# Places of results named by the planner, eight score products on eight parts of the array, and a new written order

## The chip, the core and the metric

The kernel runs on one core of a Trainium2 chip. Its engines are TensorE (PE, products; PEld is its weight load), VectorE (DVE), ScalarE (ACT), GpSimd (POOL) and SyncE (SP, which issues all the transfers here). The metric is the time of one execution in microseconds; the kernel before takes 1485.46 us (median of 3 runs, 1484.67 to 1485.84).

## The reference, cut to what matters

An attention with packed keys feeds two feed-forward layers. With 8 batches, 8 heads, 576 tokens, head size 64 and 32 packed rows:

```
def sm_attn(qq, kk, vv):
    s = scale * qq @ kk^T;  a = softmax(s);  return a @ vv
p_packed = sm_attn(p, k, v)              # 32 rows per batch and head
x = sm_attn(q, p_packed, p_packed)       # 4608 tokens x 512
h = x @ w_in;  g = (a0 + a1 h + a2 h^2 + a3 h^3) / (1 + |b0||h| + |b1|h^2 + 1e-6)
x2 = g @ w_out                           # 512 -> 2048 -> 512
h = x2 @ w_in2;  out = (h - tanh(h)) @ w_out2
```

All weights arrive as 64-bit words and are brought to two 32-bit parts (high and low) on the chip; products of the layers are three passes (high by low, low by high, high by high).

## The kernel before, in words

The first attention is done in 16 units `u` (a batch and four of its heads). A unit is a chain over engines: `sc` (scores, PE), `mx` (row maximum, DVE), `ex` (exp, ACT), `et` (transposes, PE), `ta` (ACT), `av` (times v, PE), `y` (ACT), `bt` (transposes, PE), `bd` (ACT), and `z` (the sums' reciprocals, DVE). In `sc` the keys lie with two heads in the two halves of the partitions, and 288 tokens of the 576 make one result bank: eight products of 64 rows by 32 columns of weights, four for the first half of the tokens and then four for the second, on the same four parts of the array.

The second attention is folded into the first layer: `g` multiplies the packed rows of a batch with a 256-wide piece of `w_in` (`gH`, `gL` split its result), `sm` makes the scores of a block of tokens, `si sx ss se sz sn so sh sl` their softmax and split. The tokens stand in 10 blocks of 384 or 512, each with 8 steps; step `g` (0 to 79) is `l1` (PE, hidden values), `ft fu fw` (ACT), `f2 f3` (DVE), `fq` (POOL or DVE), `r` (ACT), `b0 b1 b2` (DVE), `b3` (POOL or DVE), and the second product in two parts: `l2h` needs `b0`, `l2l` needs `b3`. The weights come as `raw` (two buffers), are turned by `d1` (ACT or DVE), `dA` (ACT) and `d` (DVE), and are split by `wh` (ACT) and `w2`, `w3`, `w4` (POOL or DVE). After the 80 steps come the last layer's products `l3`, `l4`, `m3`, `m4`.

The results of `sc et av g sm l1` take turns in a ring "h" of two places in the result memory, each two banks. `l3` opens other banks in the same memory, behind the last `f3`.

Every engine works through its own queue in order. The order of all 3965 pieces of work is written out in a table, `ORDER`, of such names (a `+` sets the second of two possible engines); a class `Plan` walks through it and issues each piece, and where the table has nothing ready it would choose by costs and due times. An entry of the table thus fixes what stands in front of it on its engine, and nothing more.

Of the kernel before, what the change touches and what calls it, by code (L numbers as in the profile page):

```python
# [26 lines left out]
v.0 v.1 k.0 k.1 p.0 raw.0.0 raw.0.1 raw.1.0 id raw.1.1 dA.0 d1.0+ q.0 d.0 raw.2.0 dA.1 sc.0 sc.1 mx.0 d1.1+ ex.0  # L27
raw.2.1 mx.1 et.0 ex.1 et.1 d.1 raw.3.0 ta.0 z.0 av.0 ta.1 y.0 av.1 dA.2 z.1 bt.0 y.1 bd.0 d1.2+ bt.1 bd.1 sm.0 c
raw.3.1 d1.3 g.0.1 d.2 si.0 sx.0 ss.0+ p.1 open_t dA.3 d.3 se.0 sz.0 gH.0.1 k.2 sn.0+ raw.4.0 raw.4.1 gL.0.1 d1.4 sc.2
g.0.0 mx.2 dA.4 ex.2 so.0 d.4 w1d.0 sh.0 gH.0.0 wh.4.0 raw.5.0 raw.5.1 sl.0+ g.0.2 gL.0.0 w2.0+ wh.4.1 dA.5 l1.0 cabs  # L30
w1d.1 w2.1+ d1.5+ gH.0.2 raw.6.0 d.5 fu.0 gL.0.2 et.2 ft.0 fw.0 z.2 f2.0 raw.6.1 f3.0 g.0.3 ta.2 raw.7.0 fq.0 l1.1 r.0
d1.6+ dA.6 ft.1 b0.0 d.6 v.2 gH.0.3 gL.0.3 wh.6.1 l2h.0 av.2 w2.3+ fu.1 f2.1 wh.6.0 raw.7.1 w2.2 fw.1 f3.1 y.2 dA.7
b1.0 fq.1+ k.3 p.2 g.0.4 gH.0.4 b2.0 b3.0 bt.2 bd.2 w1d.2 w1d.3 raw.8.0 gL.0.4 sc.3 l1.2 d1.7 mx.3 r.1 ex.3 raw.8.1
d.7 ft.2 b0.1 fu.2 w1.1.0 b1.1 d1.8+ dA.8 d.8 fw.2 f2.2 et.3 l2l.0 fq.2 raw.9.0 ta.3 f3.2 wh.8.0 l2h.1 w2.4+ raw.9.1
wh.8.1 w2.5+ l1.3 z.3 q.1 g.0.5 r.2 d1.9 b2.1 b0.2 ft.3 fu.3 dA.9 b3.1+ fw.3 raw.10.0 b1.2 f2.3 gH.0.5 d.9 f3.3
raw.10.1 fq.3 l2l.1 gL.0.5 d1.10 b2.2 l1.4 b3.2+ v.3 av.3 dA.10 k.4 d.10 raw.11.0 fu.4 ft.4 f2.4 y.3 wh.10.1 wh.10.0
l2h.2 fw.4 bt.3 bd.3 f3.4 w2.7+ r.3 w2.6+ sc.4 raw.11.1 sm.1 dA.11 mx.4 p.3 w1d.5 si.1 l2l.2 fq.4 ex.4 b0.3 raw.12.0
d1.11 b1.3 r.4 d.11 b2.3 et.4 l1.5 ta.4 fu.5 raw.12.1 k.5 ft.5 dA.12 b3.3 z.4 sx.1 f2.5 g.0.6 v.4 f3.5 gH.0.6 d1.12
ss.1 l2h.3 raw.13.0 gL.0.6 b0.4 fw.5 raw.13.1 d.12 sc.5 se.1 av.4 y.4 bt.4 w1d.7 wh.12.0 bd.4 mx.5 ex.5 l2l.3 wh.12.1
w2.8+ et.5 w1d.6 v.5 b1.4 fq.5+ l1.6 dA.13 w2.9+ sz.1 d1.13 ta.5 fu.6 b2.4 g.1.0 ft.6 gH.1.0 d.13 f2.6 gH.1.1 wh.13.0  # L40
wh.13.1 raw.14.0 gL.1.0 r.5 f3.6 z.5 b3.4 l2h.4 fw.6 g.0.7 gL.1.1 gH.0.7 av.5 w2.11 raw.14.1 w2.10+ sn.1+ fq.6 gL.0.7
so.1 y.5 dA.14 d1.14 bt.5 b0.5 d.14 k.6 l2l.4 w1d.4 v.6 bd.5 sh.1 b1.5 r.6 b2.5 sl.1 sc.6 l1.7 fu.7 ft.7 l2h.5 mx.6
wh.14.0 f2.7 f3.7 raw.15.0 raw.15.1 ex.6 b3.5+ w2.12+ et.6 d1.15 wh.14.1 l1.8 b0.6 dA.15 d.15 w1.1.2 w2.13+ fw.7 ta.6
ft.8 z.6 l2l.5 av.6 wh.15.0 wh.15.1 p.4 l2h.6 f2.8 fq.7 fu.8 y.6 w2.15+ w2.14 r.7 rx f3.8 b1.6 bt.6 fw.8 b0.7 b2.6
b1.7 fq.8+ bd.6 b3.6 l1.9 g.1.2 ft.9 f2.9 gH.1.2 fu.9 gL.1.2 gH.1.3 l2h.7 f3.9 b2.7 l2l.6 b3.7+ fw.9 fq.9+ k.7 l1.10
r.8 ft.10 l2l.7 sp.0.0 fu.10 gL.1.3 b0.8 b1.8 sp.0.1 b2.8 f2.10 fw.10 w1.1.4 l1.11 l2h.8 fq.10+ ft.11 f3.10 g.1.4
fu.11 f2.11 r.9 gH.1.4 st.0.1 f3.11 b3.8 st.0.0 b0.9 b1.9 l2l.8 q.2 w1.1.6 v.7 sc.7 gH.1.5 b2.9 r.10 l2h.9 gL.1.4
gL.1.5 fw.11 sm.2 mx.7 b3.9 fq.11 ex.7 si.2 r.11 l2l.9 et.7 sx.2 l1.12 ta.7 ft.12 fu.12 b0.10 av.7 l2h.10 b1.10 ss.2+
b2.10 fw.12 z.7 y.7 se.2 f2.12 bt.7 f3.12 b3.10 bd.7 fq.12+ r.12 sz.2 l1.13 g.1.6 b0.11 l2l.10 gH.1.6 k.8 b0.12 ft.13
fu.13 b1.11 gL.1.6 gH.1.7 fw.13 f2.13 l2h.11 sn.2 fq.13 f3.13 gL.1.7 l1.14 b2.11 r.13 b3.11+ so.2 b1.12 fu.14 l1.15  # L50
# [233 lines left out]
class Plan:  # L284

    SIGNAL = {"PE": 200, "ACT": 150, "DVE": 130, "POOL": 135}

    IDLE, WARM = 1200, 3400
    PORT = ("DVE", "POOL")

    ALT = 600
    alts = {}
# [29 lines left out]
    def run(self):  # L328
# [131 lines left out]
def packed_attention_moe_kernel(  # L460
# [622 lines left out]
    EARLY = 4  # L1083
# [938 lines left out]
```

## Time and profile before

| | |
|---|---|
| three runs, median | 1485.46 us |
| the profiled execution | 1483.95 us, span 1482.2 us, mean granted clock 0.988 |
| PE | 1436.9 us busy, 97% of the span |
| DVE | 1237.0 us, 83% |
| ACT | 897.5 us, 61% |
| POOL | 280.5 us, 19% |
| DMA | 257.87 MB, mean 174 GB/s |

The times of the working below are those of the profiled execution; 1.75 us of it lie outside the span. An average over the span hides that its stretches have different limits: the table of 40 slices on the page shows DVE at nine tenths and over from about 75 us to about 700 us, PE below that only in the first slices and once in the middle, and DMA above eight tenths in the first two slices. A time in a timeline row is that of the first instruction of the row, and the number after it how long the row's instructions took together.

### The profile page before, as it was taken

To read this page: it belongs to the slowest core of one execution; us is meant where nothing else is said; L and a number is where in the kernel's file an instruction comes from. 1 tells how busy PE (TensorE), PEld (TensorE's weight loads), DVE (VectorE), ACT (ScalarE), POOL (GpSimd) and SP (SyncE) were. 2 spreads that over 40 slices of the span, in tenths; PEclk is the share of its full clock that TensorE was granted. 3 is DMA by queue.
4 is the path that set the end of the run, shared out by engine and by line. 5 is a ranking of instruction groups with operands and counts; after the bars stand their busy time and mean duration, and the time that the engine had idled before them with its cause. 6 is when DMAs were issued, how large, how long until landed. Compare 5 with 4: busy or idle time off the path is not lost.

```text
span 1482.2 us, 21855 instructions
## 1 busy us (share of the span) xinstructions
PE 1436.9 (97%) x8448; PEld 1191.6 (80%) x8448; DVE 1237.0 (83%) x1588; ACT 897.5 (61%) x1235; POOL 280.5 (19%) x168
## 2 busy tenths in 40 slices
PE   4789999999999999999989999999999999999998
PEld 1668888877899888888978888888888888888887
DVE  4899999999999999999978876797588657977785
ACT  4898777767776777677976543454355324543353
POOL 0232322113112322333210223201220112020000
PEclk8899999999999999999999999999999999999999
DMA  8873322232331313131236889587566566575563
GB/s 299 296 255 129 131 76 98 77 144 98 131 128 58 107 57 114 58 136 43 72 122 215 238 260 335 190 296 260 199 237 229 196 221 244 197 260 199 213 210 131
DMA packets 75000, 257.87 MB, mean 174 GB/s; under 512 B 7184, under 2 KB 25744, under 8 KB 60048
## 3 DMA queue, kind: packets, MB, share of 16 engines
q1 hardware_dynamic: 74896, 256.47, 49.9%
q8 instruction: 67, 1.10, 0.3%
q14 instruction: 37, 0.30, 0.1%
HBM read 204.02 MB, written 52.43 MB: 173 GB/s over the span
## 4 chain that ended last, share of the span: by engine, by line
PE 90%; DVE 4%; ACT 3%; issue 1%; DMA 1%; SPq 0%; DVEq 0%; ACTq 0%
PE acc L961 24%; PE acc L1296 19%; PE b L1296 17%; PE h L948 13%; PE b L1081 9%; PE h L801 3%; PE acc L1121 1%; PE acc L1122 1%; PE acc L1123 1%; PE h L724 1%; PE h L769 1%; DMA raw<-in_w_dram 1%; DVE t L986 1%; PE h L754 1%; DVE m L1009 0%
## 5 line engine op out<-in xcount | busy, mean ns | idle before, releaser
L948 PE MATMUL h<-ah,slot 128*128 128x320 f32 (+3 forms) x1024 | 214.8, 304 | 0.0
L961 PE MATMUL acc<-gh,slot 128*128 128x512 f32 (+1 forms) x800 | 172.7, 367 | 0.6 <-DVE gh L1003 0.6
L948 PEld LDWEIGHTS h<-ah,slot 128*128 128x128 f32 x1024 | 170.7, 193 | 1.1
L961 PEld LDWEIGHTS acc<-gh,slot 128*128 128x128 f32 x800 | 143.5, 188 | 30.7 <-issue 10.7
L961 PE MATMUL acc<-raw,slot 128*128 128x512 f32 (+1 forms) x720 | 165.4, 379 | 0.0
L961 PEld LDWEIGHTS acc<-raw,slot 128*128 128x128 f32 x720 | 130.2, 188 | 29.9 <-issue 9.2
L948 PE MATMUL h<-al,slot 128*128 128x192 f32 (+3 forms) x512 | 150.7, 308 | 2.7 <-DVE slot L813 1.5
L1335 ACT ACTIVATE yh<-slot 128x512 fp32r<-128x512 f32 x140 | 88.2, 631 | 79.7 <-PE b L1296 25.4
L1339 DVE TENSOR_TENSOR yl<-slot,yh 128x512 fp32r<-128x512 f32 x140 | 97.9, 714 | 19.6 <-ACT yh L1335 19.0
L971 ACT ACTIVATE t<-h,coa 128x1024 f32<-128x1024 f32 (+1 forms) x80 | 89.2, 1118 | 37.9 <-PE h L948 31.8
L975 ACT ACTIVATE u<-h 128x1024 f32<-128x1024 f32 (+1 forms) x80 | 74.9, 936 | 51.8 <-PE h L948 37.9
L948 PEld LDWEIGHTS h<-al,slot 128*128 128x128 f32 x512 | 98.3, 192 | 9.5 <-issue 4.8
L986 DVE TENSOR_TENSOR t<-t,h 128x1024 f32<-128x1024 f32 (+1 forms) x80 | 88.5, 1108 | 15.2 <-ACT t L971 10.2
L990 DVE SCALAR_TENSOR_TENSOR t<-t,coa,h 128x1024 f32<-128x1024 f32 (+1 forms) x80 | 93.7, 1171 | 2.9 <-ACT u L975 1.0
L961 PE MATMUL acc<-gl,slot 128*128 128x384 f32 (+1 forms) x400 | 91.9, 372 | 2.5 <-DVE gl L1012 2.5
L983 POOL TENSOR_TENSOR m<-u,r 128x1024 f32<-128x1024 f32 (+1 forms) x27 | 58.4, 2162 | 166.3 <-DVE t L986 46.6
L1081 PE MATMUL b<-xh,slot 128*128 128x512 f32 x256 | 83.3, 399 | 6.4 <-DVE t L990 6.4
L1335 ACT ACTIVATE yh<-ex 128x512 fp32r<-128x512 f32 x84 | 53.0, 632 | 52.0 <-PE acc L1296 18.7
L961 PEld LDWEIGHTS acc<-gl,slot 128*128 128x128 f32 x400 | 72.0, 190 | 14.5 <-issue 3.6
L1296 PE MATMUL acc<-yh,rg 128*128 128x512 f32 x256 | 78.8, 389 | 0.0
L1296 PE MATMUL acc<-yh,raw 128*128 128x512 f32 x256 | 78.8, 389 | 0.0
L1296 PE MATMUL b<-slot,rg 128*128 128x512 f32 x336 | 77.5, 389 | 0.0
(218 smaller groups left out, 3259.0 us busy)
## 6 DMA issues: line engine op xcount, KB each, us to landing
raw<-in_w_dram SPq DMA_DIRECT2D x64, 512.0 KB, 4.5
w<-w1d SPq DMA_DIRECT2D x28, 1024.0 KB, 4.8
raw<-w4d SPq DMA_DIRECT2D x28, 1024.0 KB, 5.1
rg<-w4d SPq DMA_DIRECT2D x28, 1024.0 KB, 5.2
rg<-w3d SPq DMA_DIRECT2D x12, 1024.0 KB, 5.1
raw<-w3d SPq DMA_DIRECT2D x12, 1024.0 KB, 5.0
k<-in_kT_dram SPq DMA_DIRECT2D x16, 576.0 KB, 5.4
out_dram<-o SPq DMA_DIRECT2D x36, 256.0 KB, 5.6
```

The costliest lines, as they stand in the source:

```text
L801: pe.matmul(out=ps[32 * hp:32 * hp + 32, i, :], lhsT=pp[b][r, hp, :], rhs=x[r, hp, :])
L948: pe.matmul(out=ps[:, f, t], lhsT=x, rhs=y, start=(i == 0), stop=(i == len(seq) - 1))
L961: pe.matmul(out=acc_t[n][m][:, 0:XW[n]], lhsT=w2_slot[2 * p + f][:, o:o + 128], rhs=x[:, f, :], start=(p == 0 and part == 512 and f == 0), ...
L971: act.activation(out=t_t[g], in_=hv(g), func=AF.Identity, scale=a3, bias=a2)
L975: act.activation(out=u_t[g], in_=hv(g), func=AF.Abs)
L983: by.tensor_tensor(out=q_m[g], in0=u_t.pop(g), in1=r_t[g], op=ALU.mult)
L986: dve.tensor_tensor(out=t_t[g], in0=t_t[g], in1=hv(g), op=ALU.mult)
L990: dve.scalar_tensor_tensor(out=t, in0=t, scalar=a1, in1=hv(g), op0=ALU.add, op1=ALU.mult)
L1081: pe.matmul(out=hy(b, f), lhsT=a, rhs=w, start=(j == 0), stop=(j == len(seq) - 1))
L1296: pe.matmul(out=to, lhsT=a, rhs=b, start=(first and n == 0 and i in (1, 6, 7, 5)), stop=(last and n == len(seq) - 1), skip_group_check=True,)
L1335: act.activation(out=yh_t[s, i, f], in_=g_of(GSRC[i], f), func=AF.Copy)
L1339: by.tensor_tensor(out=yl_t[s, i, f], in0=g_of(GSRC[i], f), in1=yh_t[s, i, f].bitcast(F32), op=ALU.subtract)
```

## The change

Three things change.

1. `Plan` names the place that a piece of work takes in a ring. Before, rings went round in turn. Now, for all rings but that of streamed weights, it takes the place that comes free first, and the tile is made under that place's name (`h0`, `h1`; for tanh tiles `t0` to `t2`).
2. The scores of the two halves of the tokens go to different parts of the array. The second half's keys are stored with the two heads' partitions exchanged, `p` is stored twice (once exchanged, so its load goes from 64 to 128 KB), and the loop over halves is innermost. Number and size of the products stay: eight of 64 by 32 weights and 288 columns per unit.
3. `ORDER` is a new table with the same 3965 names; 169 of them change engine. The costs used where the table leaves a choice are new as well. The last 410 pieces on PE (from the fifteenth `l3` of the second block on) stand as before.

The diff, cut to its core:

```
+    TURNS = ("w",)
...
+        def place(ring):
+            held = taken[ring]
+            if len(held) < rings[ring]:
+                return 0, len(held)
+            if ring in self.TURNS:
+                held = held[:1]
+            return min(((max(end[y] for y in x), i) for i, x in enumerate(held) if all(y in end for y in x)), default=None)
...
-            if x[5] and len(taken[x[5]]) >= rings[x[5]]:
-                free = taken[x[5]][-rings[x[5]]]
-                if any(y not in end for y in free):
+            if x[5]:
+                at = place(x[5])
+                if at is None:
                     return None
...
-        bd[b] = bd_p.tile([128, 4, 32], F32, tag="bd", name="bd", bufs=2)
+        bd[b] = bd_p.tile([128, 2, 4, 32], F32, tag="bd", name="bd", bufs=2)
...
-        for c2 in range(2):
-            for r in range(2):
-                for i in range(2):
+        for r in range(2):
+            for i in range(2):
+                for c2 in range(2):
                     o = 64 * r + 32 * i
+                    rows = slice(64 * (i ^ c2), 64 * (i ^ c2) + 64)
                     pe.matmul(
                         out=ps[o:o + 32, c2, 0:HB],
-                        lhsT=bd[b][64 * i:64 * i + 64, 2 * c + r, :],
-                        rhs=k[64 * i:64 * i + 64, r, c2 * HB:(c2 + 1) * HB],
+                        lhsT=bd[b][rows, c2, 2 * c + r, :],
+                        rhs=k[rows, r, c2 * HB:(c2 + 1) * HB],
                     )
...
-        ps_t[key] = ps_h.tile([128, 2, 512], F32, tag="h", name="h")
+        ps_t[key] = ps_h.tile([128, 2, 512], F32, tag=f"h{plan.slot}", name=f"h{plan.slot}")
...
-v.0 v.1 k.0 k.1 p.0 raw.0.0 raw.0.1 raw.1.0 id raw.1.1 dA.0 d1.0+ q.0 d.0 raw.2.0 dA.1 sc.0 sc.1 mx.0 d1.1+ ex.0
+p.0 k.0 raw.0.0 sc.0 k.1 mx.0 raw.0.1 id ex.0 sc.1 v.1 mx.1 et.0 d1.0+ dA.0 ex.1 v.0 et.1 d.0 raw.1.0 raw.1.1 z.0
...
```

On SP, at the start of the program, the transfers of before stand so (`bd` is the tile of `p`, `idt` the identity):

```order
L714 DMA v<-in_va_dram 128x1024
L715 DMA v<-in_vb_dram 64x256
L714 DMA v<-in_va_dram 128x1024
L715 DMA v<-in_vb_dram 64x256
L710 DMA k<-in_kT_dram 128x1152 x2
L678 DMA bd<-in_pT_dram 128x128
L613 DMA raw<-in_w_dram 128x512 x3
L1556 DMA idt<-in_ident_dram 128x128
L613 DMA raw<-in_w_dram 128x512
L682 DMA q<-in_qT_dram 128x4x384
```

On SP at the same place, after the change:

```order
L694 DMA bd<-in_pT_dram 128x256
L726 DMA k<-in_kT_dram 128x1152
L629 DMA raw<-in_w_dram 128x512
L726 DMA k<-in_kT_dram 128x1152
L629 DMA raw<-in_w_dram 128x512
L1571 DMA idt<-in_ident_dram 128x128
L730 DMA v<-in_va_dram 128x1024
L731 DMA v<-in_vb_dram 64x256
L730 DMA v<-in_va_dram 128x1024
L731 DMA v<-in_vb_dram 64x256
L629 DMA raw<-in_w_dram 128x512 x2
L698 DMA q<-in_qT_dram 128x4x384
```

The scores' inputs moved from the fifth and sixth place to the first two, and both `v` loads behind them.

On DVE, early in the first block, before (`STREAM_TRANSPOSE q<-h` is `si` of block 0; `slot<-raw` of 1024 is `d`, `slot<-h` is `gL`; `t<-t,h` is `f2`):

```order
L634 TENSOR_SCALAR raw<-raw 128x1024
L647 SCALAR_TENSOR_TENSOR slot_78<-raw 128x1024
L827 STREAM_TRANSPOSE q<-h 128x384 x2
L838 TENSOR_REDUCE smx<-q 128x24
L842 TENSOR_TENSOR q<-q,smx 128x768
L647 SCALAR_TENSOR_TENSOR slot_79<-raw 128x1024
L850 TENSOR_REDUCE ssum<-q 128x24
L851 TENSOR_SCALAR ssum<-ssum 128x24
L852 RECIPROCAL ssum<-ssum 128x24
L856 TENSOR_TENSOR q<-q,ssum 128x768
L813 TENSOR_TENSOR slot_85<-h,slot_85 128x512
```

On DVE at the same place, after the change:

```order
L844 STREAM_TRANSPOSE q<-h_268 128x384 x2
L855 TENSOR_REDUCE smx<-q 128x24
L650 TENSOR_SCALAR raw<-raw 128x1024
L859 TENSOR_TENSOR q<-q,smx 128x768
L663 SCALAR_TENSOR_TENSOR slot_78<-raw 128x1024
L867 TENSOR_REDUCE ssum<-q 128x24
L868 TENSOR_SCALAR ssum<-ssum 128x24
L869 RECIPROCAL ssum<-ssum 128x24
L830 TENSOR_TENSOR slot_85<-h_279,slot_85 128x512
```

The third weight pair (`slot_78`) moved from before `si` to behind it, and the multiplication `sn` (L856) left DVE for POOL.

On DVE, at the end of the 80 steps, from the last but one `f3` to the last one, before (`m<-m,gh` is `b1`, `m<-u,r` is `fq`, `m<-t,coa,m` is `b2`, `gl<-m,r` is `b3`):

```order
L990 SCALAR_TENSOR_TENSOR t_304<-t_304,coa,h 128x768
L986 TENSOR_TENSOR t_305<-t_305,h 128x768
L1005 SCALAR_TENSOR_TENSOR m_311<-m_311,gh_312 128x768
L647 SCALAR_TENSOR_TENSOR raw<-raw 128x1024
L983 TENSOR_TENSOR m_310<-u_307,r_308 128x768
L1009 SCALAR_TENSOR_TENSOR m_311<-t_306,coa,m_311 128x768
L1539 TENSOR_TENSOR slot_92<-raw,slot_92 128x512
L1539 TENSOR_TENSOR slot_919<-raw,slot_919 128x512
L1012 TENSOR_TENSOR gl_313<-m_311,r_309 128x768
L990 SCALAR_TENSOR_TENSOR t_305<-t_305,coa,h 128x768
```

On DVE at the same place, after the change:

```order
L1005 SCALAR_TENSOR_TENSOR t_349<-t_349,coa,h_6563 128x768
L663 SCALAR_TENSOR_TENSOR raw<-raw 128x1024
L1020 SCALAR_TENSOR_TENSOR m_356<-m_356,gh_357 128x768
L998 TENSOR_TENSOR m_355<-u_352,r_353 128x768
L1554 TENSOR_TENSOR slot_92<-raw,slot_92 128x512
L1554 TENSOR_TENSOR slot_997<-raw,slot_997 128x512
L1024 SCALAR_TENSOR_TENSOR m_356<-t_351,coa,m_356 128x768
L1001 TENSOR_TENSOR t_350<-t_350,h_6588 128x768
L1005 SCALAR_TENSOR_TENSOR t_350<-t_350,coa,h_6588 128x768
```

The last `f2` moved from the front of this stretch to its end, and one `b3` left it.

## Rows read from the trace of the kernel before

**Rows 1.** Busy time by stretch: PE, PEld, DVE, ACT, POOL, granted clock, DMA share, GB/s.
```profile
0.00:26.07 26.07, 10.83 (x162) 5.97 (x162) 7.68 (x15) 8.86 (x18) 0.37 (x7) 0.93 0.87 297
26.07:118.74 92.67, 73.45 (x687) 56.85 (x680) 84.41 (x111) 81.93 (x119) 21.61 (x12) 0.87 0.83 280
118.74:745.00 626.26, 626.26 (x4409) 528.36 (x4407) 590.06 (x607) 463.72 (x549) 163.78 (x76) 1.00 0.27 96
745.00:757.00 12.00, 4.94 (x27) 4.14 (x25) 11.96 (x14) 10.05 (x12) 3.12 (x2) 0.84 0.29 108
757.00:1477.80 720.80, 720.80 (x3174) 596.12 (x3175) 541.47 (x843) 332.95 (x540) 91.60 (x71) 1.00 0.65 225
```
**Rows 2.** Timeline, first 27 us: start, length, engine, line; in brackets the wait.
```profile
11.23 4.07 PE L724 MATMUL h<-k,bd 64*32 64x288 f32 x32 [11.23 <-DMA bd<-in_pT_dram]
11.69 0.22 PEld L724 LDWEIGHTS h<-k,bd 64*32 64x32 f32 x4 [0.26 <-issue]
24.54 1.22 PE L801 MATMUL h<-q,pp 64*32 64x384 f32 x13
26.07 1.05 DVE L827 STREAM_TRANSPOSE q<-h 128x384 f32<-128x384 f32 x2 [0.89 <-PE h L801]
```
**Rows 3.** DVE's groups from 26.07 to 118.74 us: busy, mean ns, idle before.
```profile
L647 DVE SCALAR_TENSOR_TENSOR raw<-raw 128x1024 uint32<-128x1024 uint32 x7 | 8.5, 1216 | 0.4 <-ACT raw L642 0.3
...
L986 DVE TENSOR_TENSOR t<-t,h 128x768 f32<-128x768 f32 x8 | 7.6, 952 | 4.6 <-ACT t L971 4.6
L1539 DVE TENSOR_TENSOR slot<-raw,slot 128x512 fp32r<-128x512 f32 x11 | 7.3, 686 | 0.0
L1003 DVE SCALAR_TENSOR_TENSOR gh<-t,coa,r 128x768 fp32r<-128x768 f32 x6 | 6.2, 1026 | 1.4 <-ACT r L996 1.4
L634 DVE TENSOR_SCALAR raw<-raw 128x1024 uint32<-128x1024 uint32 x3 | 2.8, 932 | 0.0
L856 DVE TENSOR_TENSOR q<-q,ssum 128x1024 f32<-128x1024 f32 x1 | 1.2, 1212 | 0.0
```
**Rows 4.** Timeline around the low part of the sixth step, DVE and PE.
```profile
117.78 0.95 DVE L1012 TENSOR_TENSOR gl<-m,r 128x768 fp32r<-128x768 f32 x1
118.01 0.33 PE L948 MATMUL h<-al,slot 128*128 128x192 f32 x1
121.19 1.58 PE L961 MATMUL acc<-gl,slot 128*128 128x384 f32 x8
122.70 0.90 PE L769 MATMUL h<-v,ett 128*32 128x64 f32 x40
```
**Rows 5.** Timeline: one unit's scores, and products on eight parts of the array.
```profile
190.08 1.17 PE L724 MATMUL h<-k,bd 64*32 64x288 f32 x16
193.22 1.09 PE L801 MATMUL h<-w,pp 64*32 64x512 f32 x16
193.22 0.18 PEld L801 LDWEIGHTS h<-w,pp 64*32 64x32 f32 x16 [0.35 <-issue]
90.03 0.67 PE L801 MATMUL h<-slot,pp 64*32 64x256 f32 x16 [0.71 <-ACT ett L759]
```
**Rows 6.** Timeline: eight products before a full-array line, and before a small one.
```profile
732.56 1.55 PE L961 MATMUL acc<-gl,slot 128*128 128x384 f32 x8
733.94 2.94 PE L961 MATMUL acc<-gh,slot 128*128 128x384 f32 x16
109.03 1.66 PE L961 MATMUL acc<-gl,slot 128*128 128x384 f32 x8
110.63 1.18 PE L724 MATMUL h<-k,bd 64*32 64x288 f32 x16
```
**Rows 7.** Timeline at the end of the 80 steps, DVE and PE.
```profile
747.71 1.01 DVE L990 SCALAR_TENSOR_TENSOR t<-t,coa,h 128x768 f32<-128x768 f32 x1
755.84 1.00 DVE L990 SCALAR_TENSOR_TENSOR t<-t,coa,h 128x768 f32<-128x768 f32 x1
756.99 0.76 PE L1081 MATMUL b<-xh,slot 128*128 128x512 f32 x1 [6.44 <-DVE t L990]
```

More of the change, by code (lines that the diff above doesn't have):

```diff
@@ L426, in run @@
             port = x[9] and engine in self.PORT
+            if x[5]:
+                self.slot = place(x[5])[1]
             if port and self.tc:
@@ L439, in run @@
             if x[5]:
-                taken[x[5]].append([real(y) for y in x[6]])
+                held, free = taken[x[5]], [real(y) for y in x[6]]
+                if x[5] in self.TURNS:
+                    held[:] = held[len(held) == rings[x[5]]:] + [free]
+                else:
+                    held[self.slot:self.slot + 1] = [free]
             if engine == "PE":
@@ L1633, in packed_attention_moe_kernel @@
         have = [("bd", u) for b, _, _ in pieces_of(n) for u in (2 * b, 2 * b + 1)]
-        add(("sm", n), "PE", 4 * W / 2.4 - 25 + 100 * len(have) / 2, lambda n=n: sm_pe(n, ring(("s", n))),
+        add(("sm", n), "PE", 4 * W / 2.4 + 150 + 100 * len(have) / 2, lambda n=n: sm_pe(n, ring(("s", n))),
             [("q", n)] + have, d, take="h", free=[("si", n)])
@@ L1770, in packed_attention_moe_kernel @@
         add(("th", f), "ACT", AC, lambda f=f: elem(0, f, 0),
-            [("l3", 0, f)] + ([("open y",)] + [("yl", f - TT)] * (f >= EARLY + TT) if f >= EARLY else [("xl", 0, k) for k in range(4)] if f >= 2 else []),
-            e + P_E + O("th") + O("th0", f < EARLY), behind=[("th", 2)] if f == 3 else [])
+            [("l3", 0, f)] + ([("open y",)] if f >= EARLY else [("xl", 0, k) for k in range(4)] if f >= 2 else []),
+            e + P_E + O("th") + O("th0", f < EARLY), behind=[("th", 2)] if f == 3 else [],
+            **(dict(take="t", free=[("yl", f)]) if f >= EARLY else {}))
         add(("su", f), "DVE", AD, lambda f=f: elem(0, f, 1), [("th", f)], e + P_E + O("su0", f < EARLY))
@@ L1877, in packed_attention_moe_kernel, with step @@
                 add(("m3", s, j, i), "PE", 6 * MM, lambda s=s, j=j, i=i: m3(s, j, i), need, e + 0.25 * n, **kw)
-            def step(x, eng, cost, need, at, port=None, s=s, j=j):
+            def step(x, eng, cost, need, at, port=None, s=s, j=j, **kw):
                 if type(eng) is tuple:
@@ L1883, in step @@
                     run = lambda: m3_step(s, j, x)
-                add((x, s, j), eng, cost, run, need, e + 0.25 * at, port=port)
+                add((x, s, j), eng, cost, run, need, e + 0.25 * at, port=port, **kw)
             old = lambda x: [(x, s, j - 2)] if j >= 2 else [("mc12", s - 1, y) for y in range(2)]
```

559 lines of the change are left out of this document (278 added, 281 removed).

## The prediction

> **What bounds the kernel now.** I read the busy time by stretch first, since the page's 97% for PE is an average over stretches with different limits. Four limits follow each other [rows 1]. Up to 26.07 us PE works for 10.83 us and DVE for 7.68: both wait for loads, which run at 297 GB/s, and for the round trips of the first two units. From 26.07 to 118.74 DVE is busy for 84.41 of 92.67 us, ACT for 81.93, PE for 73.45: here the softmax, the turning of the weights and the chain of the first block all want DVE, and PE idles for 19.2 us behind it. From 118.74 to 745 PE is busy for all of 626.26 us, and again from 757 to 1477.80: there only fewer or shorter PE instructions bring anything. Between 745 and 757 PE has 4.94 us of work while DVE works for 11.96 of 12: the first `l3` waits 6.44 us for the last `f3` [rows 1, 7].
>
> So the time is made of the moment at which PE becomes the bound, the PE work after it, and the wait at 757. I take as that moment the start of the sixth step's `l2l` at 121.19 us, and as what can delay it the end of its `b3` on DVE at 118.73 (117.78 and 0.95) [rows 4]; in the kernel before PE itself was the later of the two, by 2.5 us.
>
> **The change, part by part.** All sums are against the profiled execution's span of 1482.20 us. The execution took 1.75 us more, 1483.95, and the median of the three runs is another 1.51 above that.
>
> *Start.* Before, the first `sc` stands behind four loads of 576 KB and `p` of 64 KB, and starts at 11.23 us, ended by the load of `p` [rows 2]. These 2.42 MB take 8.2 us at 297 GB/s [rows 1]; 3.1 us remain as issue and latency. After, `p` (128 KB) and one `k` stand in front: 0.72 MB, 2.4 us, so 5.5 us. The units' later steps need `v` (3.60 MB, 15.2 us) and block 0's `sm` needs `q` (5.44 MB, 21.4 us). Before, `sm` ran at 24.54 and DVE began its softmax at 26.07 [rows 2]. So `sm` comes 3.1 us earlier, and not 5.7: `q` is late next.
>
> *DVE up to that `b3`.* From the softmax of block 0 to the sixth `b3` the two tables have nearly the same DVE work. Only after: four `d1` of 0.93 (ACT before), three `fq` of 0.95 (POOL before; priced as the equally large L986), `ss` and `sl` of block 1 at 1.21, two `w2` of 0.69, together 10.4 us. Only before: `sn` of blocks 0 and 1 (0.95 and 1.21), three `w2` (2.1), one `b3` (0.95), two `gL` priced as the equally large L1539 (1.4), an `f2` and an `f3` (2.0), together 8.6. And the third weight pair, 0.93 and 1.22, now stands behind `si` and not in front of it. That is 4.0 us more [rows 3]. DVE's idle time in the stretch is 8.3 us [rows 1]; 4.6 us of it stood before `f2` and 1.4 before `b0` [rows 3]. I take 2.0 us of it as gone: weight steps stand where the first `f2` and `b0` waited, but there is a new wait as well, since the `d1` of the fifth weight pair now stands in DVE's queue ahead of the fourth's `d`, and its load, with 9.90 MB up to it and not 9.18, lands at 36.4 us, about 1.5 us after DVE comes there. Bounds: none of the idle time goes, or all 8.3. With the value taken the `b3` ends at 118.73 - 3.1 + 4.0 - 2.0 = 117.6 us.
>
> PE has then not yet done the `l1` that before lies from 118.01 to 121.19 (3.2 us), but has done a seventh unit's `av` (0.9) [rows 4]. The `l2l` starts at 117.7 and not 121.19, and 2.3 us more work lie behind it: the start brings 3.5 - 2.3 = 1.2 us.
>
> *Scores.* Warm, one unit takes 1.17 us for its 16 matmul records [rows 5]; the weight loads come in fours, one four after the other [rows 2]. What eight parts at once cost is in the same rows: L801, with its 16 loads inside 0.18 us, takes 0.67 us at 256 columns and 1.09 at 512 [rows 5], so 0.72 at 288 columns. That is 0.45 us a unit. Seven units stand before the sixth `l2l`, where PE waits for DVE: their 3.2 us are hidden, and worth at most that if the cover goes. Nine stand behind it: 4.1 us. Bounds: nothing, if four at a time stays the rule, and half of 1.17, 5.3 us in all.
>
> In the present scores, four products of two row halves run at once into one bank: their loads stand together and the 32 records take 4.07 us in groups of four [rows 2]. After the change each bank again takes products of both row halves, as each of the two does today, but both banks at once. The Trainium skill, TensorEngine Tiling (Array Packing), section Restrictions and Gotchas, says that different row tiles cannot access the same PSUM bank at the same time. By that rule the eight would still go in turns and the sum would lose its 4.1 us; the groups of four in the trace speak against it, and I keep the row's price.
>
> *Changes of the array's form.* Eight `l2l` products take 1.38 us to the next line's start where full-array products follow, and 1.60 where a small one follows [rows 6]: 0.22 us an entrance. The new table enters small products 80 times and not 68, of these 62 and not 56 behind the sixth `l2l`: 6 x 0.22 = 1.3 us lost. The entrances before it are covered by DVE.
>
> *The middle.* From the end of the last but one `f3` (747.71 and 1.01) to that of the last (755.84 and 1.00) DVE takes 8.1 us, and in the new order one `b3` of 0.95 less stands between them. I let the wait of 6.44 us [rows 7] shrink by 0.7 and not by all of it, since `fq` and an ACT step also stand in front of the last `f3`. Bounds: it grows by 3, or it goes (6.4).
>
> *Places by name.* With two places a turn and a choice differ only where the later result comes free first, and PE waits for no ring place from 118.74 to 745 [rows 1]. I price it at nothing; its cover is that PE is the bound there. In the second layer the last 410 PE pieces stand as before, and PE has no idle time from 757 to 1477.80 [rows 1]: nothing, with up to 3 us lost if the moved `l3` and `l4` meet late weights.
>
> *Sum.* -1.2 - 4.1 + 1.3 - 0.7 = -4.7 us: a span of 1477.5, an execution of 1479.2, and a median of 1480.8 us.
>
> **The rivals.**
> *The start and the middle clear up.* If all of DVE's 8.3 us of idle time go, the `b3` ends 6.3 us earlier than I take, and if half of the middle's wait goes as well, 2.5 more: 1480.8 - 8.8 = 1472.0. For it: DVE's waits are for ACT's results of the chain, and ACT has about 3 us less to do before the sixth step (four `d1` left it, part of another block's softmax came). Against: ACT too is busy for 81.93 of 92.67 us [rows 1].
> *The scores gain nothing.* The eight products run in two groups as now: 1480.8 + 4.1 = 1484.9. For it: one unit's loads come in fours today [rows 2], and the change sets products of both row halves on both banks at once, which no row shows. Against: the fours already mix row halves in one bank [rows 2], and L801 has its eight at once [rows 5]. The Trainium skill's rule named above (TensorEngine Tiling (Array Packing), Restrictions and Gotchas) speaks for it as well.
> *The head start is eaten by the loads.* If none of the 2.0 us of idle time goes and the late fifth weight pair costs its 1.5 us, the start loses 2.3 us and not gains 1.2: 1484.3. For it: loads run at 280 GB/s through the stretch, hardly less than the 297 at the start [rows 1]. Against: later weight pairs have as many bytes before them as now, and DVE reaches them later.
> *The attention in front starves the block (slower).* Units 3 to 6 now stand before the fourth `l2h`; DVE's share of them, with the softmax of block 1, delays that step's `b0` by 6 us of work. Each of these units hands over three times to PE, in PE's queue in order, at `et`, `av` and `bt`; such waits are in the trace with 0.71 us before L801 [rows 5]. Twelve at 0.7 are 8.4 us; with the loads' loss of 3.5 that makes 1492.7. It decides from about 6 us of such waits on, since the gains of scores and start together are that large. For it: PE's queue cannot pass a waiting `et`. Against: PE idles for 19.2 us in this stretch today [rows 1], and work of units 3 to 6 that fills such a gap is gone from later.
>
> **How the numbers follow.** The forecast's case (1475 to 1484) gets 0.50; the clearing up 0.20; the scores without gain 0.08; the eaten head start 0.11; the starved block 0.11. About 0.2%, 3.0 us, is what a measurement of this kernel can tell from no change, so faster means under 1482.5 and slower over 1488.4. Faster: 0.44 of the forecast's 0.50 and the clearing up, 0.64. Same: the rest of the forecast, the two small cases, and a little of the starved block, 0.26. Slower: 0.10. The range leaves out a tenth at each end: it reaches from the clearing up's inner half, 1470, to 1488.
>
> **What would show it.** Right: the first `sc` starts near 5.5 us, and the first block's DVE transpose near 23; a warm unit's scores take about 0.72 us with 16 loads together; DVE is busy for over nine tenths until the sixth `b3` near 117.6, and PE without a gap from there to the middle; the wait before the first `l3` is between 4 and 6.5 us. Wrong: loads of the scores that still come in fours; waits before `et`, `av`, `bt` in the first 110 us that add up to more than 6 us; a PE gap between 120 and 740 or behind 760.

## The result, and the profile after

The changed kernel takes 1472.80 us (median of 4 runs, 1470.85 to 1473.64) where the kernel before, run beside it, takes 1485.52 (1484.67 to 1485.84): a ratio of 0.9913, 95% interval 0.9896 to 0.9931. The forecast was 1480.8, with a range of 1470 to 1488. It was right in sign and range, and had little more than a third of the gain: -4.7 us forecast, -12.7 measured.

The profiled execution of the changed kernel took 1473.64 us, span 1471.9, 0.8 above its median; that of the kernel before was 1.5 below its own. So the two traces differ by 10.3 us of span, and the accounts below add up to that.

Busy time by stretch (columns as in [rows 1]), cut at these events: DVE's transposes of block 0, the end of the sixth `b3`, the start of the first `l3`, the end of the wait behind it, the end of PE's work.

```profile
0.00:21.43 21.43, 11.10 (x155) 5.75 (x162) 6.04 (x12) 7.79 (x17) 0.37 (x7) 1.00 0.93 331
21.43:112.68 91.25, 71.59 (x727) 54.39 (x712) 85.11 (x115) 76.75 (x116) 18.27 (x11) 0.91 0.85 284
112.68:743.47 630.79, 629.76 (x4402) 532.38 (x4401) 594.62 (x610) 467.20 (x553) 175.49 (x83) 1.00 0.27 98
743.47:764.91 21.44, 18.38 (x85) 15.20 (x85) 17.61 (x23) 19.71 (x25) 1.87 (x1) 0.99 0.41 134
764.91:1467.50 702.59, 702.59 (x3090) 581.46 (x3091) 526.70 (x814) 318.74 (x524) 101.59 (x85) 1.00 0.66 228
```

The shape is the same: DVE up to the sixth `b3`, PE from there on, and one break in the middle. The first stretch is 4.6 us shorter, the second 1.4, and the wait of 6.44 us in front of the first `l3` [rows 7] is gone; another of 3.07 has come 21 us behind it.

The start in the timeline, PE and DVE (the rows that answer to [rows 2]):

```profile
5.23 1.22 PE L741 MATMUL h<-k,bd 64*32 64x288 f32 x16 [5.23 <-DMA k<-in_kT_dram]
8.71 1.22 PE L741 MATMUL h<-k,bd 64*32 64x288 f32 x16 [2.26 <-DMA k<-in_kT_dram]
...
19.54 1.77 PE L818 MATMUL h<-q,pp 64*32 64x384 f32 x16 [0.41 <-ACT pp L811]
21.43 1.05 DVE L844 STREAM_TRANSPOSE q<-h 128x384 f32<-128x384 f32 x2 [0.77 <-PE h L818]
```

The sixth step's low part, DVE and PE (to [rows 4]), and a unit's scores in the stretch that PE bounds (to [rows 5]):

```profile
111.73 0.95 DVE L1027 TENSOR_TENSOR gl<-m,r 128x768 fp32r<-128x768 f32 x1
...
113.84 1.55 PE L976 MATMUL acc<-gl,slot 128*128 128x384 f32 x8
...
166.80 0.72 PE L741 MATMUL h<-k,bd 64*32 64x288 f32 x16
167.44 1.42 PE L976 MATMUL acc<-raw,slot 128*128 128x512 f32 x5
166.80 0.18 PEld L741 LDWEIGHTS h<-k,bd 64*32 64x32 f32 x16 [0.35 <-issue]
```

All 16 weight loads of a unit now stand together, and what follows starts 0.64 us after the scores.

The middle, DVE and PE (to [rows 7]):

```profile
740.94 1.01 DVE L1005 SCALAR_TENSOR_TENSOR t<-t,coa,h 128x768 f32<-128x768 f32 x1
...
747.87 1.01 DVE L1005 SCALAR_TENSOR_TENSOR t<-t,coa,h 128x768 f32<-128x768 f32 x1
...
743.47 0.39 PE L1096 MATMUL b<-xh,slot 128*128 128x512 f32 x1
...
761.17 0.69 DVE L1115 TENSOR_TENSOR s<-b,s 128x512 f32<-128x512 f32 x1 [2.83 <-ACT s L1111]
...
763.91 0.95 DVE L1027 TENSOR_TENSOR gl<-m,r 128x768 fp32r<-128x768 f32 x1
...
764.91 2.93 PE L976 MATMUL acc<-gl,slot 128*128 128x384 f32 x8 [3.07 <-DVE gl L1027]
```

The first `l3` (L1096) starts at 743.47 without a wait, in front of the last `f3` (747.87) and not behind it. That is the surprise: the last `f3`, for which it waited before, still ends 5.4 us behind the moment at which PE is free (6.3 before). The new wait is `l2l.78` for `b3.78`, which stands in DVE's queue behind a sum that waits 2.83 us for a tanh.

### The profile page after: what moved, and what is told of

Read it like the earlier page. It is cut to its first block, busy times and chain, and to the rows that moved or that the text cites. A ratio compares the mean times of both kernels' runs of the same rounds, so it can differ in the third digit from the quotient of the medians.

```text
span 1471.9 us, 21847 instructions
## 1 busy us (share of the span) xinstructions
PE 1434.1 (97%) x8448; PEld 1189.4 (81%) x8448; DVE 1231.5 (84%) x1573; ACT 890.2 (60%) x1231; POOL 297.6 (20%) x187
## 4 chain that ended last, share of the span: by engine, by line
PE 91%; DVE 4%; ACT 2%; DMA 2%; issue 1%; SPq 0%; POOL 0%; DVEq 0%; ACTq 0%; POOLq 0%
PE acc L976 25%; PE acc L1311 20%; PE b L1311 17%; PE h L963 13%; PE b L1096 8%; PE h L818 3%; DMA raw<-in_w_dram 1%; PE acc L1137 1%; PE acc L1136 1%; PE acc L1138 1%; PE h L786 1%; PE h L771 1%; DVE gh L1018 1%; DMA k<-in_kT_dram 0%; PE h L741 0%
## 5 line engine op out<-in xcount | busy, mean ns | idle before, releaser
L1001 DVE TENSOR_TENSOR t<-t,h 128x1024 f32<-128x1024 f32 (+1 forms) x80 | 88.7, 1109 | 17.3 <-ACT t L986 10.3
L1096 PE MATMUL b<-xh,slot 128*128 128x512 f32 x256 | 82.0, 396 | 0.0
L1311 PE MATMUL acc<-slot,raw 128*128 128x512 f32 x336 | 77.5, 389 | 0.0
```

The source lines that it names most:

```text
L1001: dve.tensor_tensor(out=t_t[g], in0=t_t[g], in1=hv(g), op=ALU.mult)
L1096: pe.matmul(out=hy(b, f), lhsT=a, rhs=w, start=(j == 0), stop=(j == len(seq) - 1))
L1311: pe.matmul(out=to, lhsT=a, rhs=b, start=(first and n == 0 and i in (1, 6, 7, 5)), stop=(last and n == len(seq) - 1), skip_group_check=True,)
```

## The experiments

The change has three parts that can be set one by one: the scores, the order, the places by name. The last column but one is the start of the first `l3` less its wait, so the moment at which PE is free for it, in the profiled execution; the last is the span behind that moment.

| kernel | median us | ratio, 95% | longest PE wait, 740 to 800 us | PE free | to the end |
|---|---|---|---|---|---|
| before | 1485.52 | 1 | 6.4, first `l3` | 750.6 | 731.6 |
| scores | 1480.57 | 0.9973 (0.9963 to 0.9984) | 6.4, first `l3` | 746.0 | 732.5 |
| places | 1489.02 | 1.0032 (1.0020 to 1.0045) | 6.4, first `l3` | 754.5 | 732.7 |
| order | 1483.89 | 0.9995 (0.9986 to 1.0004) | 5.4, first `l3` | 751.2 | 731.2 |
| order, scores | 1477.83 | 0.9956 (0.9942 to 0.9970) | 5.4, first `l3` | 746.5 | 731.3 |
| order, places | 1478.34 | 0.9960 (0.9948 to 0.9973) | 3.1, `l2l.78` | 750.6 | 729.6 |
| all three (changed kernel) | 1472.80 | 0.9913 (0.9896 to 0.9931) | 3.1, `l2l.78` | 743.5 | 728.4 |
| before, banks exchanged | 1480.43 | 0.9971 (0.9960 to 0.9982) | 1.4, fifth `l3` | 751.9 | 726.8 |
| scores, banks exchanged | 1477.80 | 0.9953 (0.9941 to 0.9965) | 1.4, fifth `l3` | 749.8 | 726.8 |
| order, scores, banks exch. | 1478.27 | 0.9949 (0.9935 to 0.9963) | 3.1, `l2l.78` | 747.6 | 729.9 |
| all three, banks exchanged | 1476.58 | 0.9946 (0.9933 to 0.9958) | 5.4, first `l3` | 742.9 | 730.9 |

Ratios are to the kernel before beside each run. Single executions differ by up to 4 us in the front: of kernels that are the same up to there, the one before and its exchange of banks start the sixth `l2l` at 121.19 and 122.67, the two with the new scores in the old order at 120.15 and 124.11. So a difference between two single traces in the front shows little by itself.

**Scores alone.** Old order, old ring.

```
-        for c2 in range(2):
-            for r in range(2):
-                for i in range(2):
+        for r in range(2):
+            for i in range(2):
+                for c2 in range(2):
+                    rows = slice(64 * (i ^ c2), 64 * (i ^ c2) + 64)
```

> The kernel before with the new scores alone (both halves of the tokens on different array tiles, the tables of keys and P laid out for it); its own order and its results without named places are kept. Theory: one unit goes from 1.10 to about 0.65 us from its first product to what follows it, the units behind the front give that back whole, and the time falls by 3.5 to 4.5 us (9 to 10 units of 0.46 us); the first l3 still waits 5 to 7 us for the last f3. Rival: the unit is shorter but the time is not, because the vector engine and not TensorE paces the stretch of the blocks: 0 to -1 us.

-4.0 us by the ratio (2.4 to 5.5 by its interval), as the theory had it; `l3` waits as before.

**Places by name alone.** The changed kernel's program with the old table and the old scores; against the kernel before:

```
-        ps_t[key] = ps_h.tile([128, 2, 512], F32, tag="h", name="h")
+        ps_t[key] = ps_h.tile([128, 2, 512], F32, tag=f"h{plan.slot}", name=f"h{plan.slot}")
...
-        i = len(uses) % 2
+        i = plan.slot
```

> The kernel before with the named places alone: old scores, old order on every engine; each result and tanh tile has its own place. Theory: the first l3 at 757 us waited for the last f3 only because both results of the ring were released as one; with named places it waits for the f3 before the last, which ends some 8 us earlier, so the 6.44 us in front of it fall to under 1 us and the time falls by 3 to 6 us. Nothing else moves by more than 1 us. Rival: the wait is there for the order of the work, not for the place: l3 still starts behind the last f3 and the time stays within 1 us.

Both were wrong: it is 0.32% slower, 4.8 us (3.0 to 6.7 by the interval). The wait of 6.44 us stays, and a new one comes in front, at a unit's scores (DVE, which frees the place, and PE of this kernel):

```profile
57.37 0.69 DVE L829 TENSOR_TENSOR slot<-h,slot 128x512 fp32r<-128x512 f32 x1
...
58.11 1.18 PE L740 MATMUL h<-k,bd 64*32 64x288 f32 x8 [2.14 <-DVE slot L829]
...
760.90 0.77 PE L1095 MATMUL b<-xh,slot 128*128 128x512 f32 x1 [6.44 <-DVE t L1004]
```

In the kernel before these scores waited for ACT's copy of the other place, and less:

```profile
56.19 1.17 PE L724 MATMUL h<-k,bd 64*32 64x288 f32 x16 [0.71 <-ACT pp L794]
```

The planner chooses the place that is free first by its own durations, and on the chip the other one was free first: ACT's copy out of it ended at 56.6 us, DVE's subtraction at 58.1. Then PE ran at a granted clock of 0.66 from 58 to 66 us, where the kernel before had 1.00 from 56 to 64. In this trace PE is free for the first `l3` 3.9 us later, and all of it stands ahead of the sixth `l2l` (125.10 against 121.19). That is no more than two executions of one program can differ there, so that the kernel is slower is shown by the runs' times, and that this place is the cause is argued from one trace.

**Order alone, and order with scores.** Before, a table that names a piece whose turn in the ring has not come can't be walked; here such a piece goes right behind what frees its place (three pieces on PE).

```
-            if given and given[-1][0] in ready.get(given[-1][1], ()):
-                name, engine = given.pop()
-                best = (start(engine, name), engine, name)
+            for i in reversed(range(len(given))):
+                name, engine = given[i]
+                if name in ready.get(engine, ()):
+                    t = start(engine, name)
+                    if t is not None:
+                        best = (t, engine, name)
+                        del given[i]
+                        break
```

> The new order alone, with the old scores and without named places (where the order asks for a place that is not free in turn, the piece is put right behind what frees it: three pieces on TensorE move by a few places). Theory: the start is 3 to 5 us shorter (the blocks' first l2 of the sixth group some 6 us earlier, half of it lost again), and the first l3 still waits 4 to 7 us for the last f3; the time falls by 3 to 5 us. Rival: the order is what removed the wait of the first l3 as well; then it falls by 7 to 10 us and that wait is under 1 us.

> New order and new scores together, without named places: what the change would be without them. Theory: the two add up, -7 to -9 us, with a wait of 4 to 7 us left in front of the first l3; the last 4 to 5 us of the measured gain are the named places. Rival: the named places are worth nothing (as the prediction had it), and this one is as fast as the changed kernel, -12 to -13 us.

The order alone is within its interval of nothing, and neither expectation for it came true. Its sixth `l2l` starts at 116.27 us, 4.9 earlier, but the lead is gone before the wait: PE is free for the first `l3` at 751.2, where the kernel before has 750.6. Of the 5.6 us lost in between, 2.0 are work that was still to do (3.2 of an `l1`, less 1.2 of an `av` and a `bt`) and 1.5 are small waits of PE (2.2 against 0.6); for the other 2.0 I have no row, and the prediction's 1.3 for changes of form may be in them. Had PE kept it, the lead would have ended in the wait for the last `f3`, which starts hardly sooner on DVE (755.45 against 755.84). With the scores it is -6.5 us, just short of the theory's 7, and the wait of 5.4 us stays; so the rest of the gain came with the places, which alone cost time. The programs' memory maps show which: the ring's two places are banks 4 and 5, and 6 and 7. In the kernel before, and in the one with the places alone, the last `l1` (79) holds 4 and 5, and the first `l3` is given 4 and 5. In the changed kernel the last `l1` holds 6 and 7, the first `l3` 4 and 5, which `f3.78` has left. So it is in all the kernels of this document: where the maps give the first `l3` the banks of the last `l1`, it waits 5.4 or 6.4 us; where not, it does not wait.

**The banks alone.** In the kernel before, the second layer's pairs change places; no instruction moves.

```
     banks_p.append(pool_of(ctx, "ps_b", space=PSUM))
+    for x in range(2):
+        banks_p[0].tile([128, 512], F32, tag=f"b1{x}", name=f"b1{x}")
```

> The kernel before with one thing changed: the two pairs of PSUM banks of the second layer change places, so the first l3 writes banks 6 and 7 (last held by l1.78) and not 4 and 5 (last held by l1.79). No instruction moves. Theory: the wait of 6.44 us in front of the first l3 is a matter of which banks it is given; it goes, the l3 starts right behind the l2 at 750.6 us, the vector engine behind it then sets the pace for some of it, and the time falls by 3 to 5 us. Rival: the order of the work makes that wait; the time stays within 1 us.

-4.3 us by the ratio (2.7 to 5.9), with these rows (DVE's last `f3` but one and PE):

```profile
749.18 1.01 DVE L992 SCALAR_TENSOR_TENSOR t<-t,coa,h 128x768 f32<-128x768 f32 x1
...
750.36 1.66 PE L963 MATMUL acc<-gl,slot 128*128 128x384 f32 x8
751.86 0.39 PE L1083 MATMUL b<-xh,slot 128*128 128x512 f32 x1
```

The `l3` follows the `l2` without a gap. With the order kept, the banks alone make that wait or take it away.

**The changed kernel on the other banks.**

```
+    ps_h.tile([128, 2, 512], F32, tag="h1", name="h1")
```

> The changed kernel with its two ring places on the other banks, so that the first l3 gets the banks of l1.79; named places, scores and order are all kept, no instruction moves. Theory: the first l3 waits for the last f3 again (5 to 6 us, until about 749 us), the wait of 3.07 us in front of l2l.78 goes, and the time rises by 3 to 5 us over the changed kernel, to 1476 to 1478. Rival: with named places the banks don't matter; within 1 us of the changed kernel.

1476.58: the wait is back (PE of this kernel), and 0.33% of the time is lost (the ratios, 0.9946 less 0.9913; 4.9 us, known to some 3), with every place still named.

```profile
748.31 0.76 PE L1097 MATMUL b<-xh,slot 128*128 128x512 f32 x1 [5.39 <-DVE t L1006]
```

**Banks with the other parts.** The same two lines in the kernels with the new scores, and with order and scores.

> Old order, new scores, second layer's banks in the other places. Theory: the two gains add up, -4.1 for the scores and -3 to -5 for the banks, 1475.5 to 1477.5: what the change would be worth without a new order. Rival: the vector engine takes the second gain back, since it is no sooner at the last f3; then 1480.

> New order and new scores as in the run without named places (1477.8), and the second layer's banks in the other places. Theory: of the 5.0 us that the named places brought on top of that run, some 4 are the banks and only 1 to 2 are the places in front (three pieces that had to wait for their turn): 1473.5 to 1475. Rival A: all of it is the banks, 1472.8. Rival B: the banks bring nothing without the named places, 1477.8.

With the old order the two gains come to 1477.80 (-7.0 by the ratio), just short of the theory's sum: the span behind the first `l3` is 5.7 us shorter, but PE came to it 3.8 us later in that execution. With the new order the banks alone bring 1.0 us by the ratios and not 4; rival B is the nearest. The wait at the first `l3` goes, but 3.08 us of it come back at `l2l.78`, as in the changed kernel, and 731.3 us behind the first `l3` become 729.9. The changed kernel's span is 5.6 us shorter than this one's, in three parts. In front of the sixth `l2l` it is 3.1 us ahead (113.84 against 116.94). From there to the first `l3` it gains 1.0 (small waits of 1.0 us against 2.2). Behind that it gains 1.5, and these are no effect of the names: the wait at `l2l.78` is as long in both, but behind it the lower clock lasts 6.3 us here and 3.2 there (last section), and the changed kernel with the old scores, which has the names, has 729.6. The front's part is not settled: with the new scores, four executions with named places have the sixth `l2l` between 112.3 and 113.8 and the two without at 115.6 and 116.9; with the old scores it is 116.15 and 116.27. In the medians, the names are worth 5.5 us with the right banks and 1.3 without; each of the four differences that the banks and the names make with the new order and scores is known to some 3 us.

**The loads' order alone.** In the old table:

```
-v.0 v.1 k.0 k.1 p.0 raw.0.0 raw.0.1 raw.1.0 id raw.1.1
+p.0 k.0 raw.0.0 k.1 raw.0.1 id v.1 v.0 raw.1.0 raw.1.1
```

> The kernel before with the order of its first ten loads alone taken from the changed kernel (P and the keys first, v behind). Theory: the first scores start at 5.5 and not 11.2 us, but the q of block 0 and the first weights land no earlier, so the first block's products start 0 to 3 us earlier, and at the end 0 to 2 us are left. Rival: the early loads carry the whole gain of the new order's start (the sixth l2 starts 5 us earlier, as with the whole new order), and the time falls by 2 to 4 us.

1484.77 against 1485.34, ratio 1.0001 (0.9992 to 1.0010): nothing. PE and ACT of that run:

```profile
5.31 2.15 PE L724 MATMUL h<-k,bd 64*32 64x288 f32 x16 [5.31 <-DMA k<-in_kT_dram]
...
16.51 1.14 ACT L642 ACTIVATE raw<-raw 128x1024 f32<-128x1024 f32 x1 [5.07 <-DMA raw<-in_w_dram]
17.55 0.73 ACT L740 ACTIVATE k<-h,mx 128x576 f32<-128x576 f32 x1
...
18.42 2.40 PE L754 MATMUL h<-idt,k 128*128 128x128 f32 x10 [7.31 <-ACT k L740]
```

The scores start 5.9 us earlier, but the exp behind them (L740) stands in ACT's queue behind a weight step that waits for its load until 16.51. With the old order of ACT and DVE the early loads bring nothing; what they bring in the new one has no run of its own.

**The changed kernel with the old scores.** The loop of the first diff, put back.

> The changed kernel with the old scores, new order and named places kept. Theory: the scores are worth what they were in the old order, 4.1 us, so 1476.5 to 1477.5. Rival: with the blocks no longer paced from the front every unit counts, and then some of the front too (a unit of 1.8 to 2.1 us at the low clock goes to 1.2): 5.5 to 6.5 us, 1478.3 to 1479.3.

1478.34: by the ratios the scores are worth 0.47% here, 7.0 us, and 4.0 in the old order; the first difference is known to some 3 us, the second to 1.6. The median lies where the rival has it. But one of the five executions took 1482.03, the other four 1477.95 to 1478.89, and the trace is that of the slow one: its PE is free for the first `l3` 7.1 us later, 2.3 of it before the sixth `l2l` (116.15 against 113.84), which is within the scatter there. The pair without named places gives 0.39%, 5.8 us (0.9995 less 0.9956). Both differences are larger than 4.0, neither clearly; that units before that `l2l` count too is possible and not shown.

**Two tries at the wait that is left.** First, `b3.78` ahead of the sum that waits, and DVE's weight steps behind `b3.79`.

```
-b2.78 th.1 wh.21.0 su.1 l3.0.4 wh.21.1 w4.4+ w3.6+ b0.79 b3.78+ dA.22 d1.22 raw.23.0 b1.79 th.2
-raw.23.1 d.22 th.3 b2.79 wh.22.0 l2l.78 wh.22.1 b3.79+ l2h.79 l2l.79
+b2.78 b3.78+ th.1 wh.21.0 su.1 l3.0.4 wh.21.1 b0.79 dA.22 d1.22 b1.79 b2.79 th.2
+th.3 l2l.78 b3.79+ w4.4+ w3.6+ raw.23.0 raw.23.1 d.22 wh.22.0 wh.22.1 l2h.79 l2l.79
```

> The changed kernel with one stretch of the vector engine's order changed (seven instructions around 758 to 770 us): the residual step b3.78 goes ahead of the second sum of the second layer (which waits 2.83 us for a tanh), and the weight sums and the shift behind it go behind b3.79. Theory: the wait of 3.07 us in front of l2l.78 goes, nothing behind it has slack to give it back, and the time falls by 2.5 to 3.1 us below the changed kernel, to about 1470. Rival: TensorE waits as long one piece later (for b1.79 or b3.79, or for a weight that now comes later): within 0.7 us of the changed kernel, 1472.8.

1475.16 us, ratio 0.9934 (0.9921 to 0.9948), no better than the changed kernel. `l2l.78` no longer waits; the seventh `l3` does (`l3.0.6`, which the next expectation calls the sixth), for a sum on DVE (L1115) that now stands behind a late load:

```profile
770.51 0.69 DVE L650 TENSOR_SCALAR raw<-raw 128x1024 uint32<-128x1024 uint32 x1 [1.77 <-DMA raw<-in_w_dram]
...
772.88 0.68 DVE L1115 TENSOR_TENSOR made<-b,made 128x512 f32<-128x512 f32 x1
...
773.61 0.80 PE L1096 MATMUL b<-xh,slot 128*128 128x512 f32 x1 [4.71 <-DVE made L1115]
```

The weight steps that I had pushed back free the buffer of the next load; with them left in place (the next run), the same step starts at 769.06 without a wait. So, second: those stay, the sums that free the banks move up, and one `l3` fills PE.

```
-b2.78 th.1 wh.21.0 su.1 l3.0.4 wh.21.1 w4.4+ w3.6+ b0.79 b3.78+ dA.22
+b2.78 b3.78+ th.1 wh.21.0 su.1 l3.0.4 wh.21.1 w4.4+ w3.6+ b0.79 dA.22
...
-l2l.78 wh.22.1 b3.79+ l2h.79 l2l.79 w4.5+ w3.7+ dA.23 sp.9.0 d1.23+ raw.24.0 su.3 d.23
+l2l.78 l3.0.5 wh.22.1 b3.79+ su.3 su.2 l2h.79 l2l.79 w4.5+ w3.7+ dA.23 sp.9.0 d1.23+ raw.24.0 d.23
...
-st.9.0 su.2 open_y wh.23.0 w4.6 l3.0.5 yh.1
+st.9.0 open_y wh.23.0 w4.6 yh.1
```

> The changed kernel with three pieces moved in the stretch from 758 to 775 us, and the loads' conversions left where they were: b3.78 ahead of the second tanh sum on the vector engine, the third and fourth sums (which free the places of l3.0.2 and l3.0.3) right behind b3.79, and l3.0.5 between l2l.78 and l2h.79 on TensorE. Theory: the 3.07 us in front of l2l.78 go and the place that the sixth l3 waited for 4.71 us in the run before is free in time; with l4.0 waiting 0 to 1.5 us for its first input, 2.5 to 4 us below the changed kernel, 1469 to 1470. Rival: this stretch is paced by the loads of the second layer's weights and what the vector and scalar engines do with them, so each wait taken away comes back at the next piece: 1472 to 1475.

1469.04 us (1468.61 to 1470.52), ratio 0.9901 (0.9885 to 0.9918): the fastest of all. By the ratios it is 0.12% under the changed kernel, inside what the two intervals leave open; by the spans behind the first `l3` it is 2.9 us shorter, 725.5 against 728.4. One wait is left there, for `l4`'s first input:

```profile
766.66 1.28 DVE L1115 TENSOR_TENSOR made<-b,made 128x512 f32<-128x512 f32 x2
...
775.82 0.47 PE L1136 MATMUL acc<-yl,slot 128*128 128x512 f32 x1 [1.36 <-DVE yl L1121]
```

## Why the prediction was right in sign and short in size

**Start: forecast -1.2, measured -5.3; the mis-sized terms are DVE's work, by 3.3 us, and the loads, by 1.5.** The working had the sixth `b3` end at 118.73 - 3.1 + 4.0 - 2.0 = 117.6. Measured it is 118.73 - 4.64 + 0.70 - 2.12 = 112.7. The idle time gone (8.26 to 6.14 us) is what I took. The softmax of block 0 comes 4.6 us earlier and not 3.1, since the loads ran at 331 GB/s and not at 297: 5.44 MB and the same 3.1 us for issue give 19.5, where `sm` stands. DVE's work is 85.11 us against 84.41 [rows 1], not 4 more. Of these 3.3 us, 2.0 are the price of `d1`, taken as 0.93 us from three of the kernel before [rows 3]; eight of them now cost 0.69. Most of the rest is one `w2` less than I had counted (0.7) and a cheaper `d` for the slots (1.22 us, 1.30 before; 0.4 in all). DVE from 21.43 to 112.68 us:

```profile
L1001 DVE TENSOR_TENSOR t<-t,h 128x768 f32<-128x768 f32 x7 | 6.6, 946 | 2.2 <-ACT t L986 2.0 <-ACT u L990 0.3
...
L650 DVE TENSOR_SCALAR raw<-raw 128x1024 uint32<-128x1024 uint32 x8 | 5.4, 691 | 0.1
```

From there the sixth `l2l` starts 7.35 us earlier. Then 3.2 us of an `l1` are still to do, and 1.2 of an `av` and a `bt` are done, so 5.3 are left. That `l1` was in the forecast, the `bt` was not.

**Scores: forecast -4.1, measured -4.0** in the nine units behind that point (9.8 us to 5.8, each to the line that follows), and -4.0 in the run of its own. The price, 0.72 us from [rows 5], is the measured one to the hundredth. The Trainium skill, TensorEngine Tiling (Array Packing), section Restrictions and Gotchas, says that different row tiles cannot access the same PSUM bank at the same time (PSUM is the result memory); by that, the eight products of both row halves on both banks would have gone in turns. The trace does not agree: the 16 loads in 0.18 us and the 0.64 us to what follows say that the rule does not bind here. Whether units in front count as well, which the forecast had as "hidden, and worth at most that if the cover goes", the runs leave open.

**Changes of form: +1.3**, not measured by itself. PE is free for the first `l3` 7.1 us earlier; -5.3, -4.0 and +1.3 make -8.0; 0.4 us of the difference are small waits between the sixth `l2l` and there (1.0 against 0.6), and 0.5 stay without a row.

**The middle and the places by name: forecast -0.7 and nothing, measured -3.2.** This is the step that failed. The 3.2 us are, but for 0.2, the wait of 6.44 us that went less the one of 3.07 that came. I looked for the wait's end in DVE's order, where the last `f3` indeed comes no sooner, and priced the names at nothing because PE "waits for no ring place from 118.74 to 745". The one place that mattered is opened at 757: it was ended by an `f3`, which is the release of a place, so [rows 7] said that a place was waited for. What has to be asked of such a row is which banks. The chosen names turned the last `l1` and the first `l3` onto different banks by the way; exchanging the banks in the old kernel gains 4.3 us with nothing else changed, and exchanging them back in the new one loses 4.9. With the wait back, the changed kernel has 730.9 us to the end where the one before has 731.6: 0.8 less, so the part that I took from DVE's order was of the right size. The names themselves, with an order not made for them, cost 4.8. Whether in the new order they bring anything beyond the banks is open: without names, the right banks brought 1.0 there.

**The rivals.** The time came out at that of "the start and the middle clear up" (1472.0), which had 0.20, but neither half came by its mechanism. The sixth `b3` ended 4.9 us earlier than I took, by faster loads and less work on DVE, while DVE's idle time fell by 2.1 us, as forecast, and not by 8.3; the middle went by the banks. This rival set the lower end of the range, so that the time fell inside it was in part luck. "The scores gain nothing" is ruled out. In the run with the loads' order alone the head start came to nothing, though in ACT's queue and not at the fifth weight pair, as "the head start is eaten by the loads" has it. "The attention in front starves the block" did not happen: PE's waits for `et`, `av`, `bt` are there, but PE's idle time up to the sixth `b3`, from the windows, is 10.3 and 19.7 us against 15.2 and 19.2.

## What to carry to other kernels

Where an instruction waits for the release of a buffer, look up which buffer it was given before looking at the order: two lines that exchange two pairs of banks were worth as much as the whole change of the scores. A planner that names places by its own durations is only as good as these; with an order made for it it gained (part of that by the banks), with another it lost. And a lead at one point of one engine is not yet a gain: 4.9 us at the sixth `l2l` were gone when PE came to the first `l3`, in work left over, small waits and a rest without a row. Waits taken from the middle came back at a later piece (6.4 us as 3.1, 3.1 as 4.7) until the sums that free the banks were moved too, which left 1.4.

## What the hardware showed that I had not expected

A wait of PE can cost more than its length. After the 3.07 us in the changed kernel the granted clock is 0.50, the lower level of 1.2 GHz, for 3.2 us, and the eight products that follow take 2.73 us to the next line, where 1.4 to 1.5 is usual. The windows are the wait, what follows, and what follows that:

```profile
761.80:764.90 3.10, 0.04 (x1) 0.00 (x0) 3.10 (x6) 3.10 (x5) 0.00 (x0) 0.96 0.26 69
764.90:768.10 3.20, 3.19 (x10) 3.19 (x11) 3.10 (x4) 1.67 (x4) 0.00 (x0) 0.50 0.67 264
768.10:771.50 3.40, 3.40 (x21) 3.40 (x20) 3.40 (x6) 1.11 (x2) 0.00 (x0) 1.00 0.15 30
```

How long the lower clock lasts is not given by the wait. Behind one as long, in the kernel with order, scores and exchanged banks, it is 0.50 for 6.3 us (769.0 to 775.3), and the 16 products that follow the eight take 4.4 us to the next line where the changed kernel has 3.0. The changed kernel with the old scores has 4.3 there, with the order and the names of the changed kernel; so it is not the names, and what decides it stays open.

```profile
769.03 0.69 PE L969 MATMUL acc<-gl,slot 128*128 128x384 f32 x1 [3.08 <-DVE gl L1020]
```

After the 4.71 us of the first try at the middle it is 0.58 over the 4.9 us behind; in the last kernel, whose only wait there is 1.36 us, it is 1.00 from 774 to 780 us, on both sides of the wait.
